# Two-token loads and 128-column unpacking for two more tiles, and fewer, wider filler products

## The chip, the cores and the metric

The kernel runs on one core of a Trainium2 chip. The metric is the device time of one execution in microseconds, as the median of several runs. A core has five engines that work side by side and wait for each other by semaphores: PE (TensorE, matrix products), DVE (VectorE), ACT (ScalarE), POOL (GpSimd) and SP (SyncE, which here issues all DMAs).

## The reference

The inputs are q, k and v (8 batches, 8 heads, 576 tokens, 64 columns per head, float32) and the weights w_in (512 x 1024), conv_w (3 x 1024) and w_out (1024 x 512), which arrive as float64. Attention is computed in chunks of 64 tokens, each chunk with itself alone; a gated feed-forward part with a convolution over three tokens follows.

```python
scores = scale * np.matmul(q_c, k_c.transpose(0, 1, 2, 4, 3))     # chunks of 64 tokens
scores = scores - np.max(scores, axis=-1, keepdims=True)
attn = np.exp(scores)
attn = attn / (np.sum(attn, axis=-1, keepdims=True) + 1e-09)
x = np.matmul(attn, v_c)                                          # then heads side by side: (B, S, 512)

h = np.maximum(x @ w_in, 0.0)
conv_out = sum(conv_w[k] * hp[:, k:k + S, :] for k in range(3))   # hp: h with a zero row at each end
gate = 1.0 / (1.0 + np.exp(-conv_out))
out = (h * gate) @ w_out
```

## The kernel before

The 4608 tokens are cut into 36 tiles of 128 tokens for attention (two chunks each) and into units of about 384 tokens for the feed-forward part. Float32 accuracy on PE is reached by splitting operands into a high and a low half (names ending in `_h` and `_l`); the weights are split on the chip from their 64-bit words, in blocks: conv_w, then w_in in six loads, then w_out in four. Each block passes through one of two slots (`w_slots`), and a slot is free again when DVE has run `w_words` (L567) on it.

**A tile's way.** For the first nine tiles SP loads 128 rows of q and of k (`load_rows`) into one of three row slots. `t_pe` brings them onto PE with the head's columns on the partitions, into two PSUM banks, one call for each `i` of 0 and 1; `t_copy` copies each bank to `qkT` in SBUF, on ACT or DVE (helper lines L76 and L78). A row slot is free after its tile's second `t_pe`. Then follow `scores` (L247), the row maximum and the subtraction on DVE (L257, L261), the exponential on ACT (L266), sum and reciprocal on DVE, the normalisation, `p_pe` (four transposes, L326), `p_copy`, and `attn_v` (L339). `x_hi` (ACT) and `x_lo` (DVE) make the input of the first product `mm1` (L408). ReLU, convolution and gate follow on ACT and DVE (L416 to L481), and the second product runs at L512, in seven part products for each pair of output tiles.

**Two kinds of row loads.** For the first `NP` tiles the rows are loaded with two tokens side by side: even partitions hold q and odd ones k, partition 2p and 2p+1 tokens 2p and 2p+1 of all heads, in pieces of 512 bytes. Here `t_pe` can't transpose; it multiplies 64 columns of the rows (one head, one of the two tokens) with every second column of the identity, so that only q or only k comes out (L196). The other tiles, `NP` to 8, are loaded in pieces of 256 bytes (L133) and transposed (L201).

**What sets the order.** The program lists some 1900 steps. Each step has an engine, an assumed cost and the steps and buffers that it needs. A list written out by hand (`order_`) gives the order on every engine; a planner walks through it and assigns each step a begin in planned microseconds. The instructions are then emitted by planned begin, and each engine keeps its own order. On PE, up to a planned time of 110, gaps of the plan are filled: before a PE step, so many transposes of the identity into an idle PSUM bank are emitted as the planned gap divided by 0.14 (L1140). `pe_free` starts at 2.0, so the first gap is the one before the first `t_pe`. Only the number of fillers depends on the plan; on the chip a step starts when its engine has come to it and its semaphores are there. On the queue of SP the DMAs are issued in the same fixed order, and a DMA that waits for a slot holds back those behind it.

Of the kernel before, what the change touches and what calls it, by code (L numbers as in the profile page):

```python
# [21 lines left out]
F32R = mybir.dt.float32r  # L22
# [8 lines left out]
def attn_ffn(ctx: ExitStack, tc: tile.TileContext, q, k, v, w_in, conv_w, w_out, out):  # L31
    nc = tc.nc
    B, H, S, D = q.shape
    DM, DF = w_in.shape
    w_in, conv_w, w_out = (w.bitcast(U32) for w in (w_in, conv_w, w_out))
    P = 128
# [3 lines left out]
    G = H // 2  # L40
# [13 lines left out]
    ONE_PAIR = True  # L54
    TP = 12
    NF = 3
    NP = 5
    DIRECT = ()
    scale = 1.0 / float(D) ** 0.5

    const = ctx.enter_context(tc.tile_pool(name="const", bufs=1))
# [12 lines left out]
    def copy_on(eng, out, in_):  # L74
        if eng == "ACT":
            nc.scalar.copy(out=out, in_=in_)  # L76
        else:
            ENG[eng].tensor_copy(out=out, in_=in_)  # L78

    def step(eng, cost, key, fn, args=(), after=(), take=(), free=(), lag=0.0, port=False, bank=None, other=(), soft=()):  # L80

        s = dict(eng=eng, cost=cost, key=key, fn=fn, args=args, after=[a for a in after if a], take=take, free=free,
                 lag=lag, port=port, bank=bank, other=other, soft=[a for a in soft if a])
        steps.append(s)
        return s

    sx = ps_s.tile([P, 2, 512], F32, name="sx_ps")
    banks = [None] * 6  # L90
    ps_y = ExitStack()
    ident = const.tile([P, P], F32, name="ident")
    make_identity(nc, ident)
    rebias = const.tile([P, 1], F32, name="rebias")
    nc.scalar.activation(out=rebias, in_=ident[:, 0:1], func=AF.Exp)
    nc.gpsimd.memset(rebias, -896.0 * 2 ** 23)
# [89 lines left out]
    def t_pe(st, i):  # L186

        if not i:
            st["qk"] = work.tile([P, 2, G, 2 * C], F32, name="qkT")
        tp = banks[st["tp", i]]  # L190
        if st["t"] < NP:
            r = row_slot(st).rearrange("p (g u e d) -> p g u e d", g=G, u=2, e=2)
            for g in range(G):
                for e in range(2):
                    for u in range(2):
                        nc.tensor.matmul(tp.rearrange("p (g e n) -> p g e n", g=G, e=2)[D * u:D * u + D, g, e],  # L196
                                         lhsT=r[:, g, u, e], rhs=ident[:, i::2], start=True, stop=True)
            return
        rows = row_slot(st)[:, 512 * i:512 * i + 512]
        for g in range(G):  # L200
            nc.tensor.transpose(out=tp[:, P * g:P * g + P], in_=rows[:, P * g:P * g + P], identity=ident)  # L201

    def t_copy(st, i, eng):
        tT = st["qk"][:, i]
        if st["t"] < NP:
            copy_on(eng, tT.rearrange("p g (n e) -> p g e n", e=2), banks[st["tp", i]].rearrange("p (g e n) -> p g e n", g=G, e=2))
            return
        copy_on(eng, tT, banks[st["tp", i]].rearrange("p (g i) -> p g i", i=P))

# [481 lines left out]
    def att(t, key, load_key, writes):  # L691

        st = {"t": t}
        if t < NAT:
            r = "slot"
            ld = step("SP", 1.2 if (2 * t) % NCK < NCK - 1 else 2.3, load_key, load_rows, (st, t), take=[(r, st)], lag=1.9 if t < NP else 2.8)
            tt = []
            for i in range(2):
                s = step("PE", 0.9 if t < NP else 0.44, key - 3, t_pe, (st, i), [ld, before.get("t")], take=[("bk", st, ("tp", i))] + ["qk"] * (not i), free=[r] if i else [])
                before["t"] = s  # L700
                tt.append(step("ACT", 0.63 if t < NP else 0.59, key - 3, t_copy, (st, i), [s], free=[("bk", ("tp", i))], other=[("DVE", 0.69, False)]))
            slot_users.append(s)
        else:
            tt = [step("DVE", 1.23 if (2 * t + 1) % NCK else 1.39, key - 3, t_dve, (st, t), ring(t), take=["qk"])]
            before["T", t] = tt[0]
        ldv = step("SP", (1.7 if (2 * t) % NCK < NCK - 1 else 2.2) if t < TP else 0.5 if (2 * t) % NCK < NCK - 1 else 1.0, load_key + 0.05 if t < 5 else key - 8, load_v, (st, t), [before.get("v")], take=["v"], lag=1.1 if t < TP else 0.75 if (2 * t) % NCK < NCK - 1 else 1.2)
        tt[0]["after"] += [before["T"]] if t else []
        before.update(v=ldv, T=tt[-1])
        before["new"].append((st, t, tt, ldv, writes, key))
        if t >= PAIR and (t - PAIR) % 2 == 0:  # L710
            return
        new, old = before["new"], before["x"] if t >= BOTH else []
        before["new"], key = [], new[0][5]
        after = [a for n in new for a in n[2]] + [before.get("s")] + [a for o in old for a in o[2]]
        take = x_take(old) + s_take(new)
        free = ["qk"] * len(new) + x_free(old)
        if old:
            s = step("PE", 0.47 * len(new + old), key, both, (new[0][0], [n[0] for n in new], [o[0] for o in old]), after,
                     take=take, free=free, bank="sx")
        else:  # L720
            s = step("PE", 0.47, key, scores, (st,), after, take=take, free=free, bank="sx")
        before["s"] = s
        x_all(old, s, key)
        if t == PAIR - 1:
            a = step("POOL", 0.0, key, give_up, (lent,), [s], take=[("bk", lent, ("y", 0))])
            step("POOL", 0.0, key, give_up, (lent,), [a], take=[("bk", lent, ("y", 1))], free=[("sp", "l1")])
        if t == PAIR + 1:
            step("POOL", 0.0, key, lend, (lent,), [s], take=["sx", "sx"], free=[("sp", "l0")])
        before["x"] = [(st_, t_, end_ + [v_], w_) for (st_, t_, _, v_, w_, _), end_ in zip(new, soft_all(new, s, key))]
        if t + 1 < BOTH:  # L730
            x_alone(key + 14)
        elif t == NT - 1:
            x_alone(key + 18)
# [69 lines left out]
    group_loads, before, lent = {}, {"new": [], "x": []}, {}  # L803
# [133 lines left out]
    for u in range(NU):  # L937
# [4 lines left out]
        while begun < NT and not all(t in x_done for t in range(until[u])):  # L942
            t, begun = begun, begun + 1
# [188 lines left out]
    for i in range(6):  # L1132
        banks[i] = (early_banks if i in (lent["y", 0], lent["y", 1]) else ps_b).tile([P, 512], F32, name=f"b{i}_ps")
    made = {}
    pe_free, until_ = 2.0, 110.0
    for i in sorted(order_, key=lambda i: begin[i]):
        if steps[i]["eng"] == "PE" and begin[i] <= until_:
            idle = [b for b, uses in enumerate(taken) if all(t1 < pe_free or t0 >= begin[i] for t0, t1 in uses)]
            for _ in range(int((begin[i] - pe_free) / 0.14) if idle else 0):
                nc.tensor.transpose(out=banks[idle[-1]][:, 0:P], in_=ident, identity=ident)  # L1140
            pe_free = begin[i] + steps[i]["cost"]
        n = len(nc.cur_bb.bb.instructions) if steps[i]["port"] else 0
        steps[i]["fn"](*steps[i]["args"], *([steps[i]["eng"]] if steps[i]["other"] else []))
        if steps[i]["port"]:
            made[i] = list(nc.cur_bb.bb.instructions)[n:]
# [40 lines left out]
```

## Time and profile before

| | |
|---|---|
| time, median of 3 runs | 476.48 us (476.42 to 477.97) |
| span of the profiled execution | 475.5 us, first to last instruction; no other time of this execution is recorded |
| PE busy | 464.0 us (98%) |
| DVE, ACT, POOL busy | 413.0, 257.7, 289.4 us (87%, 54%, 61%) |
| chain that ended last | PE 89%, DVE 5%, ACT 2%, issue 2% |
| TensorE's granted clock | 0.996 on average over the span |

A busy share says how much of the span an engine worked, not whether it was waited for. The chain is followed back from the last instruction: at each step to what released it, or to the instruction before it on its engine. "Issue" is time in which an engine waited for nothing that the profile shows. The granted clock is given as a share of 2.4 GHz; the lower level, 0.50, is 1.2 GHz. Products are pipelined on PE, so that the duration of one is longer than the distance to the next; the chain's rows give the distance.

### The profile page before, as it was taken

To read this page: it belongs to the slowest core of one execution; us is meant where nothing else is said; L and a number is where in the kernel's file an instruction comes from. 1 tells how busy PE (TensorE), PEld (TensorE's weight loads), DVE (VectorE), ACT (ScalarE), POOL (GpSimd) and SP (SyncE) were. 2 spreads that over 40 slices of the span, in tenths; PEclk is the share of its full clock that TensorE was granted. 3 is DMA by queue.
4 is the path that set the end of the run, shared out by engine and by line. 5 is a ranking of instruction groups with operands and counts; after the bars stand their busy time and mean duration, and the time that the engine had idled before them with its cause. 6 is when DMAs were issued, how large, how long until landed. Compare 5 with 4: busy or idle time off the path is not lost.

```text
span 475.5 us, 13438 instructions
## 1 busy us (share of the span) xinstructions
PE 464.0 (98%) x5481; PEld 452.9 (95%) x5481; DVE 413.0 (87%) x775; ACT 257.7 (54%) x535; POOL 289.4 (61%) x260
## 2 busy tenths in 40 slices
PE   8989889999999999999999999999999999999996
PEld 8879889999999999999999999999999999999996
DVE  2869999999999898989988999898998998788694
ACT  2557989955555463554564465453545545444631
POOL 0124678976777666767667857467868553633523
PEclk9989999999999999999999999999999999999999
DMA  6878999998789999999938283600361100101002
GB/s 195 237 216 255 282 207 193 188 162 205 133 143 211 200 204 160 157 228 165 221 80 149 60 208 80 166 23 23 102 167 45 46 23 2 46 1 68 8 38 112
DMA packets 186369, 64.33 MB, mean 135 GB/s; under 512 B 159660, under 2 KB 177092, under 8 KB 186308
## 3 DMA queue, kind: packets, MB, share of 16 engines
q1 hardware_dynamic: 186308, 63.48, 61.9%
q8 instruction: 43, 0.70, 0.6%
q14 instruction: 18, 0.15, 0.1%
HBM read 50.88 MB, written 23.59 MB: 157 GB/s over the span
## 4 chain that ended last, share of the span: by engine, by line
PE 89%; DVE 5%; ACT 2%; issue 2%; POOL 1%; POOLq 0%; DVEq 0%
PE b_ps L512 38%; PE b_ps L408 38%; PE sx_ps L247 3%; PE sx_ps L339 3%; PE b_ps L196 2%; PE b_ps L1140 2%; PE z_ps L339 1%; DVE wt L567 1%; PE z_ps L247 1%; PE b_ps L326 1%; DVE gt L451 1%; DVE wt L562 1%; DVE m L257 1%; ACT wt L558 0%; DVE wt L261 0%
## 5 line engine op out<-in xcount | busy, mean ns | idle before, releaser
L512 PE MATMUL b_ps<-wo_h,f 128*128 128x256 f32 x1008 | 190.6, 282 | 0.1
L512 PEld LDWEIGHTS b_ps<-wo_h,f 128*128 128x128 f32 x1008 | 158.6, 188 | 2.2 <-POOL f L78 0.7
L512 PE MATMUL b_ps<-wo_l,f 128*128 128x256 f32 x504 | 141.3, 280 | 0.6 <-issue 0.6
L451 DVE SCALAR_TENSOR_TENSOR gt<-b_ps,cw,gt 128x384 f32<-128x384 f32 (+3 forms) x208 | 116.6, 576 | 9.0 <-ACT gt L446 7.1
L499 POOL TENSOR_TENSOR f<-gt,f 128x512 fp32r<-128x512 f32 x71 | 91.8, 1298 | 29.3 <-ACT f L76 9.8
L512 PEld LDWEIGHTS b_ps<-wo_l,f 128*128 128x128 f32 x504 | 94.9, 188 | 0.3 <-issue 0.3
L408 PE MATMUL b_ps<-x_h,wi_h 128*128 128x386 f32 (+2 forms) x384 | 84.7, 342 | 0.9 <-DVE gb L481 0.9
L408 PE MATMUL b_ps<-x_l,wi_h 128*128 128x386 f32 (+2 forms) x384 | 83.3, 338 | 0.0
L408 PE MATMUL b_ps<-x_h,wi_l 128*128 128x386 f32 (+2 forms) x384 | 83.1, 338 | 0.0
L462 ACT ACTIVATE gt<-gt 128x384 f32<-128x384 f32 (+2 forms) x96 | 50.2, 523 | 43.8 <-DVE gt L451 43.6
L408 PEld LDWEIGHTS b_ps<-x_l,wi_h 128*128 128x128 f32 x384 | 68.8, 188 | 0.0
L408 PEld LDWEIGHTS b_ps<-x_h,wi_l 128*128 128x128 f32 x384 | 68.6, 188 | 0.0
L408 PEld LDWEIGHTS b_ps<-x_h,wi_h 128*128 128x128 f32 x384 | 65.7, 188 | 1.8 <-DVE gb L481 1.2
L446 ACT ACTIVATE gt<-b_ps,cw 128x384 f32<-128x384 f32 (+2 forms) x104 | 56.4, 555 | 18.0 <-DVE b_ps L418 16.3
L416 ACT ACTIVATE b_ps<-b_ps 128x386 f32<-128x386 f32 (+2 forms) x78 | 37.3, 479 | 51.5 <-PE b_ps L408 47.6
L502 POOL TENSOR_TENSOR gt<-gt 128x512 f32<-128x512 f32 x43 | 55.5, 1295 | 15.2 <-PE b_ps L408 6.0
L481 DVE SCALAR_TENSOR_TENSOR gt<-gt,b_ps 128x192 f32<-128x192 f32 (+2 forms) x120 | 47.2, 410 | 8.1 <-ACT gt L462 7.4
L78 POOL CAST f<-gt 128x512 fp32r<-128x512 f32 x42 | 25.8, 613 | 33.9 <-PE b_ps L512 24.1
L76 ACT CAST f<-gt 128x512 fp32r<-128x512 f32 x43 | 26.5, 617 | 25.2 <-PE b_ps L512 14.8
L217 DVE STREAM_TRANSPOSE qkT<-qk 128x1024 f32<-128x1024 f32 (+1 forms) x30 | 33.3, 1119 | 0.4 <-DMA qk<-rows 0.4
L524 ACT ACTIVATE wt<-b_ps 128x256 f32<-128x256 f32 x50 | 18.9, 381 | 24.9 <-PE b_ps L512 24.9
L499 POOL TENSOR_TENSOR f<-gb,f 128x512 fp32r<-128x512 f32 x14 | 18.1, 1294 | 17.8 <-ACT f L76 8.7
(96 smaller groups left out, 614.8 us busy)
## 6 DMA issues: line engine op xcount, KB each, us to landing
out<-wt SPq DMA_DIRECT2D x36, 256.0 KB, 3.7
qk<-rows SPq DMA_DIRECT2D x24, 320.0 KB, 5.0
rows<-in_k SPq DMA_DIRECT2D x12, 576.0 KB, 8.7
rows<-in_q SPq DMA_DIRECT2D x12, 576.0 KB, 8.3
qk<-rows SPq DMA_DIRECT2D x24, 256.0 KB, 4.5
v<-in_v SPq DMA_DIRECT2D x21, 256.0 KB, 5.0
w<-in_moe_w_out SPq DMA_DIRECT2D x4, 1024.0 KB, 6.1
wt<-wt SPq DMA_DIRECT2D x48, 64.0 KB, 2.0
```

The costliest lines, as they stand in the source:

```text
L76: nc.scalar.copy(out=out, in_=in_)
L78: ENG[eng].tensor_copy(out=out, in_=in_)
L217: nc.vector.transpose(out=to[:, :, i:i + n], in_=of[:, :, o:o + n])
L408: nc.tensor.matmul(h_ps[:, 0:w], lhsT=wt[:, f // 2, kt, P * (f % 2):P * (f % 2) + P], rhs=xt[:, u % NX, kt, 0:w], start=n == 0, stop=n == ...
L416: nc.scalar.activation(out=h, in_=h, func=AF.Relu)
L446: nc.scalar.mul(out=g, in_=h, mul=cw[:, FT + f:FT + f + 1])
L451: nc.vector.scalar_tensor_tensor(out=g, in0=h, scalar=w, in1=g, op0=ALU.mult, op1=ALU.add)
L462: nc.scalar.activation(out=g, in_=g, func=AF.Tanh, scale=0.5)
L481: nc.vector.scalar_tensor_tensor(out=o, in0=g, scalar=1.0, in1=hv, op0=ALU.add, op1=ALU.mult)
L499: ENG[eng].tensor_tensor(out=part(st, 1), in0=quarter(*src), in1=part(st, 0).bitcast(F32), op=ALU.subtract)
L502: ENG[eng].tensor_tensor(out=quarter(*out_), in0=quarter(*a), in1=quarter(*b), op=op)
L512: nc.tensor.matmul(o, lhsT=part(ft, a)[:, j, :], rhs=w[:, i, j, :], start=first and n == 0, stop=n == 3 * FT // 2 - 1, skip_group_check=True)
```

## The change

Five things change. `NP` goes from 5 to 7, so tiles 5 and 6 are loaded and unpacked like tiles 0 to 4. A product of `t_pe` takes all 128 columns of the identity, reordered so that q's rows come first and then k's; one product so gives a head's q and k for one token of each pair, half of the products suffice, and a call `i` covers two pairs of heads for q and k, where before it covered all heads for q or for k. `t_copy` follows that layout. A constant `ident_r`, the identity in the format of PE's faster float32 products, is made by a copy on ACT. The fillers become products of `ident_r` (two of 256 columns, or one of 512 once 13 steps are emitted); the first gap is filled only up to a planned length of 2.9, and later gaps only where they are longer than 0.8. The list `order_` is as it was; one assumed cost of `t_pe` becomes 0.86, and the assumed cost and load delay of tiles 5 and 6 follow `NP`.

```diff
-    NP = 5
+    NP = 7
+    HALVES = 13
...
+    ident_r = const.tile([P, P], F32R, name="ident_r")
+    nc.scalar.copy(out=ident_r, in_=ident)
...
-            for g in range(G):
-                for e in range(2):
-                    for u in range(2):
-                        nc.tensor.matmul(tp.rearrange("p (g e n) -> p g e n", g=G, e=2)[D * u:D * u + D, g, e],
-                                         lhsT=r[:, g, u, e], rhs=ident[:, i::2], start=True, stop=True)
+            for n in range(4):
+                for u in range(2):
+                    nc.tensor.matmul(tp[D * u:D * u + D, P * n:P * n + P], lhsT=r[:, 2 * i + n // 2, u, n % 2],
+                                     rhs=ident.rearrange("p (n i) -> p i n", i=2), start=True, stop=True)
...
-            copy_on(eng, tT.rearrange("p g (n e) -> p g e n", e=2), banks[st["tp", i]].rearrange("p (g e n) -> p g e n", g=G, e=2))
+            copy_on(eng, st["qk"][:, :, 2 * i:2 * i + 2, :].rearrange("p i g (n e) -> p g e i n", e=2),
+                    banks[st["tp", i]].rearrange("p (g e i n) -> p g e i n", g=2, e=2, i=2))
...
-                s = step("PE", 0.9 if t < NP else 0.44, key - 3, t_pe, (st, i), [ld, before.get("t")], take=[("bk", st, ("tp", i))] + ["qk"] * (not i), free=[r] if i else [])
+                s = step("PE", 0.86 if t < NP else 0.44, key - 3, t_pe, (st, i), [ld, before.get("t")], take=[("bk", st, ("tp", i))] + ["qk"] * (not i), free=[r] if i else [])
...
-    pe_free, until_ = 2.0, 110.0
+    pe_free, until_, filled = 2.0, 110.0, 0
...
-            for _ in range(int((begin[i] - pe_free) / 0.14) if idle else 0):
-                nc.tensor.transpose(out=banks[idle[-1]][:, 0:P], in_=ident, identity=ident)
+            gap = begin[i] - pe_free if idle else 0.0
+            for _ in range(int((min(gap, 2.9) - 0.3) / 0.43) if pe_free == 2.0 else int((gap - 0.3) / 0.235) if gap > 0.8 else 0):
+                n = 2 if filled < HALVES else 4
+                for _ in range(4 // n):
+                    nc.tensor.matmul(banks[idle[-1]][:, 0:P * n], lhsT=ident_r,
+                                     rhs=ident_r.rearrange("p (o n) -> p o n", o=1).broadcast_to([P, n, P]), start=True, stop=True)
+                filled += 1
```

## Rows read from the trace of the kernel before

**Rows 1.** The page's busy times (us, share of the span) and instructions.
```profile
PE 464.0 (98%) x5481; PEld 452.9 (95%) x5481; DVE 413.0 (87%) x775; ACT 257.7 (54%) x535; POOL 289.4 (61%) x260
```

**Rows 2.** Windows: PE, PEld, DVE, ACT, POOL busy; clock, DMA share, GB/s.
```profile
0.00:18.60 18.60, 17.24 (x352) 15.56 (x354) 9.42 (x21) 5.31 (x10) 2.69 (x9) 1.00 0.72 209
...
0.00:23.34 23.34, 21.98 (x475) 19.61 (x476) 13.24 (x29) 8.64 (x16) 2.69 (x9) 1.00 0.77 216
...
23.34:25.15 1.81, 0.00 (x1) 0.00 (x0) 1.36 (x3) 0.00 (x0) 0.00 (x0) 1.00 0.51 110
25.15:28.70 3.55, 3.55 (x65) 2.98 (x65) 0.00 (x0) 2.63 (x6) 0.94 (x1) 0.53 0.73 200
28.70:78.00 49.30, 45.32 (x581) 42.44 (x583) 47.59 (x85) 42.19 (x85) 27.91 (x27) 1.00 1.02 239
78.00:470.00 392.00, 391.24 (x4353) 386.11 (x4354) 349.97 (x658) 204.25 (x431) 257.90 (x225) 1.00 0.57 116
```

**Rows 3.** The chain that ended last, in order of time: start, us, what.
```profile
1.36 5.73 PE b_ps L1140 x35
7.09 1.09 PE b_ps L196 x32
8.18 0.26 PE b_ps L1140
...
10.87 0.62 PE sx_ps L247 x32
...
23.34 1.81 issue
...
26.03 1.04 PE b_ps L326 x4
...
27.50 1.11 PE sx_ps L247 x32
28.70 0.70 DVE m L257
...
87.27 0.44 PE b_ps L326 x4
87.70 1.42 PE b_ps L512 x12
89.12 0.11 PE b_ps L1140
```

**Rows 4.** DVE's waits in 0 to 30: us in total, times, longest.
```profile
DVE m L257 <- PE sx_ps L247: 5.9, 3, 4.0
```

**Rows 5.** Timeline of PE: start, duration, what, idle before and its releaser.
```profile
25.15 0.88 PE L339 MATMUL sx_ps<-p_all,v 64*64 64x64 f32 x26 [1.81 <-issue]
...
33.38 2.35 PE L1140 MATMUL b_ps<-ident 128*128 128x128 f32 x20
...
64.53 0.69 PE L339 MATMUL sx_ps<-p_all,v 64*64 64x64 f32 x32 [1.51 <-ACT p_all L76]
```

**Rows 6.** DMA queue of kind instruction: whole span, then 22.6 to 22.8 (packets, MB, share).
```profile
q8 instruction: 43, 0.70, 0.6%
...
q8 instruction: 1, 0.02, 28.9%
```

**Rows 7.** Windows, columns as in rows 2, around two stretches of row loads.
```profile
3.00:3.50 0.50, 0.50 (x4) 0.50 (x3) 0.00 (x0) 0.00 (x0) 0.00 (x0) 1.00 1.13 339
...
22.00:22.50 0.50, 0.50 (x19) 0.50 (x21) 0.50 (x3) 0.50 (x2) 0.00 (x0) 1.00 1.26 287
```

**Rows 8.** Timeline of the first loads and of ACT's start.
```profile
1.56 0.64 SPq L126 DMA_DIRECT2D qk<-in_k  x1
2.02 0.20 ACT L95 ACTIVATE rebias<-ident 128x1 f32<-128x1 f32 x1
```

**Rows 9.** DMA issues of 1.5 to 2.2: size, us from issue to landing.
```profile
qk<-in_k SPq DMA_DIRECT2D x1, 256.0 KB, 3.3
```

**Rows 10.** All fillers on PE: duration in ns, min/median/max, first and last start.
```profile
L1140 PE MATMUL b_ps<-ident x112: 271/273/472, 1.4 to 93.7; 128*128 128x128 f32 x112
```

## Prediction, made before the change was run

> **What bounds the kernel now.** I read the shares of the engines first: PE is busy for 464.0 of 475.5 us [rows 1]. That is an average, so I took the span by stages [rows 2]. The reader is to see three regimes. From 78 to 470 us PE has no idle time that counts (391.24 of 392.00): every microsecond by which this stretch begins earlier is a microsecond of the total. From 28.7 to 78 DVE is the full engine (47.59 of 49.30), while PE has gaps and fillers. Before 28.7 neither is full: DVE did 14.6 us of work (13.24 + 1.36), all of it after conv_w landed at 5.55, and of the three times that it waited for scores, 5.9 us in all, the longest, 4.0 us, lies directly before 28.70, where the fourth scores end [rows 3, 4]. So the total is set by when that fourth scores run, and the chain of waits says what they stood behind: 5.73 us of fillers from 1.36, unpacking products with fillers between them, and 1.81 us from 23.34 in which PE waited for nothing that is recorded [rows 3].
>
> **That 1.81 us halt** is in the middle of attn_v of tile 0, whose operands were all ready (its remaining 26 products start together at 25.15 with no releaser but "issue" [rows 5]). One queue of kind "instruction" moved 43 packets, 0.70 MB, so 16 KB each [rows 6]; PE ran 5481 + 5481 instructions [rows 1], which is 255 per packet. At the halt PE had run 475 products and 476 weight loads [rows 2]; with some 7% of semaphore instructions, which are not counted, that is 1024 = 4 x 256, a packet's edge. A packet of that queue moved in 22.6 to 22.8 [rows 6], where the DMA engines were full (share 1.26 just before [rows 7]). I read it as PE waiting for its next block of instructions. Afterwards the granted clock is down: 0.53 on average until 28.70 [rows 2], where four transposes took 1.04 us and one scores 1.11 us, against 0.44 and 0.62 at full clock [rows 3].
>
> A rule speaks against this reading. The Trainium skill (Runtime: NRT & Kernel Launch, Instruction fetch mechanics) also has blocks of 256 instructions, but says that the fetch of the next runs beside the present one and is mostly hidden, and gives PE room for 2048. By that page the halt would not be a fetch, the change would not remove it, and the time would be that of rival 1. The trace agrees on the size of a block and disagrees on the hiding, as far as a halt on an edge shows it.
>
> **The change part by part**, against the span of 475.5 us; the runs' median, 476.48, lies 0.97 above it, which I add at the end.
>
> *First fill.* Before, 35 transposes hold PE from 1.36 to 7.09, though the second half of tile 0's rows (issued 1.56, 3.3 us to landing) is there at 4.9 [rows 8, 9]. Afterwards the fill is int((2.9 - 0.3)/0.43) = 6 steps of two 256-column products. They read ident_r, an ACT copy that takes its place behind the table load, where ACT's first operation now starts at 2.02 and takes 0.20 [rows 8], so PE begins near 2.35 instead of 1.36. A 256-column product takes 0.118 us at full clock (12 in 1.42 [rows 3]) and twice that at the lower level, at which the first transposes ran (up to 472 ns against a median of 273 [rows 10]). Fill: 1.4 to 2.8 us, end 3.8 to 5.2. Unpacking starts between 4.9 (rows) and 5.2; I take 5.2: **-1.8 us**. If the first unpacking product group still runs at the lower level it costs up to 1.1 us more; part of that is hidden, because DVE is busy with conv_w until 7.14 and copies tile 0 only then.
>
> *Unpacking products.* Per half tile 16 products of 64 columns (32 records, 1.09 us [rows 3]) become 8 of 128 (16 records). If the record sets the pace (34 ns), 0.55 us; if the columns do, 1.09. I take 0.95, nearer to the row of this same function: ten halves, -1.4 us. Between the halves there are thirteen small fillers in eight places up to 23 us; one costs 0.26 us on the chain, and the eight places together 2.5 us [rows 3]. Their gaps are below 0.8 us in the plan (n fillers mean 0.14n to 0.14(n+1)), so they go. That is 3.9 us of PE's own time; not all passes. With unpacking from 5.2, tile 0's copies follow conv_w's work on DVE (7.14 to 8.5), so its scores start at 8.6 instead of 10.80. Slot 0 is free at 7.4 instead of 9.5, so tile 3's rows, which wait for it, go 2.1 us earlier and tile 4's about 3 us. Following DVE's and ACT's fixed order from there with the durations of before, attn_v of tile 0 begins at 19.7 instead of 23.01: **-3.3 us, the first term included**.
>
> *The halt.* Until the end of the fourth scores the new program has 12 + 10 x 16 + 4 x 32 + 1 + 8 + 32 = 341 products, 732 instructions with the same 7%, not 1024. The fourth edge moves to about the sixth scores; there PE had 2.35 us of fillers [rows 5], a cover. An edge (768) falls just behind the fourth scores, but its packet is asked for about 6 us ahead, where before PE consumed a block in 4.7 us (18.6, where 352 + 354 had run, to 23.34 [rows 2]). So -1.81 for the halt and, with the clock kept, -0.38 - 0.60 - 0.49 - 0.43 = -1.9 for the rest of attn_v, four transposes, the scores and two fillers. That makes -7.0 at the fourth scores. DVE can't take it all: 14.6 us of work after 5.55 ends at 20.15 at best, plus waits for tile copies and w_in; I put its row-maximum at 22.7 instead of 28.70: **-6.0 us** (bounds: -8.5 from DVE's work, -3.3 if the halt stays).
>
> *28.7 to 78.* DVE's chain shifts as a whole, and what it waits for shifts with it, since the w slots are freed by DVE and the row slots by PE. Not everything can: a w_in block takes 5 to 8 us from issue to landing. Each half of tiles 5 and 6 goes from four transposes (0.44 us, as the four of [rows 3]) to 0.55 to 1.09: four times +0.5, beside gaps of which the largest held twenty fillers [rows 5]; if that cover is gone, +2 us at worst. Their copies keep 512 columns each and are costed at nothing; ACT and DVE would have to carry what they cost more. Their loads go as pieces of 512 bytes; tile 0's, of that kind, moved at 339 GB/s, the 256-byte pieces around 22 us at 287 [rows 7], so about 0.5 us less for 1.05 MB. I take **+0.8 us** given back (0 to +6).
>
> *After 78.* The gaps near 89 and 93.6 held one and two fillers, 0.11 us each on the chain of a full PE [rows 3]: **-0.3 us**.
>
> Sum: -6.0 + 0.8 - 0.3 = -5.5; span 470.0, time **471.0 us**. Its own range is 469 to 473.
>
> **Rivals.**
> 1. *The halt stays or comes back on the chain* (at another edge, or because it was no fetch). For it: the DMA stays busy (0.75 to 1.02 by stages [rows 2]), and a block took 4 us from edge to packet (18.6 to 22.6). Against it: the edge moves by some 280 instructions and the program consumes them more slowly. Then only the -3.3 and the -0.3 are left, less 0.6 given back: 473.5.
> 2. *The front's gain is lost between 28.7 and 78*: a DVE at 97% beside a DMA share of 1.02 [rows 2] may have its own end, where loads come late or the longer unpacking of tiles 5 and 6 sits before mm1. For it: the chain there passes through ACT and POOL as well, and loads of 5 to 8 us lie beside it. Against: loads wait for slots there, not for the DMA. About -1.2: 475.3.
> 3. *Slower: PE at the lower clock through the whole front.* The gaps below 0.8 us are no longer filled; before, one idle time of 1.81 us was followed by 0.50. If the level stays low from 5.2 to the fourth scores, ten halves cost 0.95 more each, three scores 0.49, and with the transposes and attn_v the fourth scores begin near 30.5, not 27.43: +3, time 479.5. It decides from about seven halves at the low level (6 / 0.95). Against: PE stays some 80% busy there, and a gap of 1.51 us at 63 was followed by an attn_v of 0.69 us, its full-clock time [rows 5].
>
> **How the numbers follow.** Forecast 0.53, more than forecast (below 469) 0.04, rival 1 0.20, rival 2 0.15, rival 3 0.08. 0.5% is 2.4 us, about what a measurement of this kernel can tell from no change; the limits are 474.1 and 478.9. Faster: 0.53 + 0.04 + 0.14 of rival 1 = 0.71. Slower: 0.07 of rival 3 and 0.02 of rival 2 = 0.09. Same: 0.20. The range, 468 to 476.5, holds forecast, rival 1 and most of rival 2.
>
> **What would show it.** First unpacking product at 4.9 to 5.3; PE idle nowhere above 1.2 us between 5 and 25 us, clock 1.00 in 8 to 30; scores of the first tile near 8.6; DVE's fourth row-maximum at 22 to 23.5; PE without gaps from about 72.5. It is wrong if a halt with "issue" stands before that row-maximum, if the clock shows 0.50 there, or if the row-maximum is early and PE's full stretch still begins at 77 or later.

## The result and the profile after

The changed kernel took 473.19 us (median; 472.39 to 476.98), the kernel before 477.23 beside it: a ratio of 0.9899 with a 95% interval of 0.985 to 0.9948, so it is faster, by 1.0% or 4.0 us. Two more sets of runs, `a_again` and `a_late` below, with the same program up to 460 us, gave 472.47 (ratio 0.9892, 0.9853 to 0.993) and 473.07 (0.9894, 0.9857 to 0.9932), 5.4 and 4.8 us below the kernel before beside them (477.83 both times). The forecast was 471.0, 5.5 us below 476.48.

The profiled execution has a span of 470.6 us, 4.9 less than before. First the front, by PE's timeline of the changed kernel (start, duration, what, and in brackets the idle time before it and its releaser; L198 is now the unpacking, L250 the scores, L342 attn_v, L1146 the fillers):

```profile
2.37 2.93 PE L1146 MATMUL b_ps<-ident_r 128*128 128x256 f32 x12 [2.37 <-ACT ident_r L96]
5.30 3.66 PE L198 MATMUL b_ps<-ident,qk 128*64 128x128 f32 x48
8.90 0.69 PE L250 MATMUL sx_ps<-qkT 64*64 64x64 f32 x32
...
17.61 2.04 PE L198 MATMUL b_ps<-ident,qk 128*64 128x128 f32 x32
20.17 0.69 PE L342 MATMUL sx_ps<-p_all,v 64*64 64x64 f32 x32 [0.53 <-ACT p_all L77]
20.80 0.66 PE L329 MATMUL b_ps<-ident,wt 128*128 128x128 f32 x4
21.57 0.69 PE L250 MATMUL sx_ps<-qkT 64*64 64x64 f32 x32
...
27.61 2.37 PE L1146 MATMUL b_ps<-ident_r 128*128 128x256 f32 x14
29.91 0.46 PE L250 MATMUL sx_ps<-qkT 64*64 64x64 f32 x15
31.22 0.50 PE L250 MATMUL sx_ps<-qkT 64*64 64x64 f32 x17 [0.86 <-issue]
```

The first fill ends where the rows are there, each of the first scores comes earlier, attn_v of tile 0 runs in one piece (0.69 us, against 6 and 26 products with 1.81 us between them [rows 3, 5]), and the halt now stands inside the sixth scores, after 15 of its 32 products. (From here on a record is one product in the trace, and a halt is idle time of PE with "issue" as its releaser.) DVE's timeline shows the fourth row-maximum with no wait before it:

```profile
22.40 0.69 DVE L260 TENSOR_REDUCE m<-sx_ps 128x8 f32<-128x512 f32 x1
```

It was at 28.70 [rows 3]. By windows (columns as in rows 2), DVE is as full as before in the next 50 us, and PE nearly without gaps from 72.80 (389.80 of 392.20 us):

```profile
5.30:22.40 17.10, 15.61 (x334) 13.50 (x334) 14.43 (x31) 8.27 (x17) 1.90 (x2) 1.00 0.97 277
...
22.40:72.80 50.40, 45.84 (x618) 41.29 (x614) 47.91 (x87) 43.92 (x89) 29.41 (x27) 1.00 1.01 242
72.80:465.00 392.20, 389.80 (x4318) 384.96 (x4318) 349.47 (x656) 203.32 (x430) 257.15 (x225) 1.00 0.57 116
```

The gain is followed by pairing the n-th product of `mm1` and of the second product in both traces: -5.78 us at 73 us, -6.15 from 92 to 127, -6.49 at 147, -5.83 at 167, -4.79 at 182, and -4.9 from there to the end. So the front was won, and 1.7 us were given back between 147 and 182 us. PE's waits of the changed kernel from 100 to 460 (total, times, longest) say where:

```profile
PE sx_ps L342 <- DVE p_all L319: 1.3, 1, 1.3
PE z_ps L342 <- DVE p_all L319: 1.0, 1, 1.0
```

`p_dve` (L319) itself waited for four small DMAs, `wt<-wt`, that swap blocks of the softmax's results between partitions; in this document "the first swap" is the one near 150 us and "the second" the one some 20 us later. SP's timeline (start, time for the issue) of the changed kernel, and then of the kernel before:

```profile
147.43 0.60 SPq L154 DMA_DIRECT2D rows<-in_k  x1
148.20 5.48 SPq L316 DMA_DIRECT2D wt<-wt  x4
```

```profile
151.11 0.65 SPq L151 DMA_DIRECT2D rows<-in_k  x1
154.69 3.16 SPq L313 DMA_DIRECT2D wt<-wt  x4
```

Before, the swap was issued 2.9 us after the issue ahead of it had ended; now it follows within 0.2 us, and the four issues take 5.48 us instead of 3.16. It still begins 6.49 us earlier, by as much as PE is ahead there; what is longer is the DMA itself, whose first piece lands 5.7 us after its issue instead of 3.4.

### The profile page after: what moved, and what is told of

Same layout as the page of the kernel before. It is cut to its first block, busy times and chain, and to the rows that moved or that the text cites. A ratio compares the mean times of both kernels' runs of the same rounds, so it can differ in the third digit from the quotient of the medians.

```text
span 470.6 us, 13056 instructions
## 1 busy us (share of the span) xinstructions
PE 456.2 (97%) x5290; PEld 444.3 (94%) x5290; DVE 412.7 (88%) x775; ACT 257.2 (55%) x536; POOL 289.3 (61%) x260
## 4 chain that ended last, share of the span: by engine, by line
PE 78%; DVE 9%; DMA 3%; POOL 3%; ACT 3%; issue 2%; SPq 2%; DVEq 0%; POOLq 0%; ACTq 0%
PE b_ps L411 34%; PE b_ps L515 34%; PE sx_ps L342 2%; DMA w<-in_moe_w_in 2%; PE sx_ps L250 2%; DVE gt L454 1%; DVE wt L570 1%; DMA wt<-wt 1%; PE z_ps L250 1%; PE z_ps L342 1%; SPq L129 1%; POOL wt L310 1%; PE b_ps L329 1%; PE b_ps L1146 1%; SPq L316 1%
```

## The experiments

Theory A was the prediction's: the front sets the time, and the halt is PE's wait for its next block of instructions. The rivals: C, the first fill is what counts; D, the row loads of tiles 5 and 6; others as quoted. "At 100 us" means the shift of the paired products there, against the first trace of before.

**Products alone** (`b_products`), the kernel before with the new `t_pe` and `t_copy`:

```diff
...
-                        nc.tensor.matmul(tp.rearrange("p (g e n) -> p g e n", g=G, e=2)[D * u:D * u + D, g, e],
-                                         lhsT=r[:, g, u, e], rhs=ident[:, i::2], start=True, stop=True)
...
+                    nc.tensor.matmul(tp[D * u:D * u + D, P * n:P * n + P], lhsT=r[:, 2 * i + n // 2, u, n % 2],
+                                     rhs=ident.rearrange("p (n i) -> p i n", i=2), start=True, stop=True)
...
```

> The kernel before with one edit alone: unpacking by 128-column products (16 records per half tile instead of 32); five tiles, loads and fillers as before. Theory A (the 1.81 us halt is PE at the edge of a 256-instruction block that has not arrived): PE runs 160 records fewer before attn_v of tile 0, so the edge that lay at its seventh record lies about 33 us in, among fillers; no halt of over 0.5 us before the fourth scores, clock 1.00 in 20 to 30, the fourth row-maximum on DVE near 24.2 instead of 28.7, time 3 to 4.5 us below the kernel before (about 472.5). Theory B (the halt is no fetch): it stays in attn_v of tile 0, the gain is ten times 0.11 us and less, time within 1.2 us of the kernel before.

477.63 us (475.34 to 479.75), ratio 0.9983 (0.9956 to 1.001): no gain. There was no halt in the front, as Theory A said, and Theory B falls with that; but the time is what Theory B said. The fourth row-maximum came at 26.26, not near 24.2, the products at 100 us were only 1.6 us earlier, and in the profiled execution (479.45, one of the slowest of the twelve) all of that was lost again: the last products are 2.2 us later than before. PE's waits from 100 to 460 in that profile:

```profile
PE z_ps L339 <- DVE p_all L316: 1.7, 1, 1.7
PE sx_ps L339 <- DVE p_all L316: 1.3, 1, 1.3
PE z_ps L247 <- issue: 0.8, 1, 0.8
PE b_ps L408 <- issue: 0.5, 1, 0.5
```

**Fillers alone** (`b_fill`), the kernel before with `ident_r` and the new filler rule:

```diff
...
-            for _ in range(int((begin[i] - pe_free) / 0.14) if idle else 0):
...
+            for _ in range(int((min(gap, 2.9) - 0.3) / 0.43) if pe_free == 2.0 else int((gap - 0.3) / 0.235) if gap > 0.8 else 0):
...
```

> The kernel before with one edit alone: the new fillers (ident_r, first fill of 12 products of 256 columns, later ones in long gaps alone); unpacking and loads as before. Both theories: first unpacking product at 5.3 instead of 7.0. Theory A: only 36 records go before attn_v, so the edge lies in the fourth scores, about 9 of 32 records in, and a halt of 0.5 to 2 us stands there, with a low clock behind it if it is long; time 1.5 to 3 us below the kernel before. Theory B (the halt came from the fillers or from something in attn_v): no halt in the fourth scores; either none at all, with 4 us or more below the kernel before, or one in attn_v as before.

477.97 us (476.38 to 480.22), ratio 0.9989 (0.996 to 1.0017): no gain, where Theory A had 1.5 to 3 us. In the profiled execution (476.48, one of the fastest) the front was 3.35 us earlier at 100 us in spite of three halts; 1.6 us went in a swap wait at 177.5 and 1.8 in a halt at 255.8. PE's timeline of the front:

```profile
11.87 0.50 PE L250 MATMUL sx_ps<-qkT 64*64 64x64 f32 x17 [0.34 <-DVE qkT L79]
12.96 0.46 PE L250 MATMUL sx_ps<-qkT 64*64 64x64 f32 x15 [0.59 <-issue]
16.31 0.46 PE L250 MATMUL sx_ps<-qkT 64*64 64x64 f32 x16
17.34 0.46 PE L250 MATMUL sx_ps<-qkT 64*64 64x64 f32 x16 [0.57 <-issue]
22.02 0.34 PE L250 MATMUL sx_ps<-qkT 64*64 64x64 f32 x6 [0.19 <-ACT x_h L397]
23.92 0.62 PE L250 MATMUL sx_ps<-qkT 64*64 64x64 f32 x26 [1.56 <-issue]
```

The last of them stands in the fourth scores, after 6 of its products, where Theory A had about 9. Each halt is inside a group of equal products whose operands are there. Counted from the start of the program they stand after 222, 349 and 475 records of products: 127 and 126 apart. So many products and as many weight loads are 252 to 254 instructions, 256 if two to four semaphore instructions, which are not counted, stand among them.

**More records in the first gap** (`b_shift`): three of the first transposes become eight small products (two records each), 13 records more ahead of attn_v.

```diff
-            for _ in range(int((begin[i] - pe_free) / 0.14) if idle else 0):
+            for _ in range(int((begin[i] - pe_free) / 0.14) - 3 * (pe_free == 2.0) if idle else 0):
...
+            for n in range(8 if pe_free == 2.0 else 0):
+                nc.tensor.matmul(banks[idle[-1]][D * (n % 2):D * (n % 2) + D, 0:D], lhsT=ident[:, 0:D], rhs=ident[:, 0::2], start=True, stop=True)
```

> The kernel before with 13 more records of PE in its first gap (3 transposes out, 8 small products of 2 records in; about 0.2 us longer), nothing else. Theory A: the edge comes 13 records earlier, so the halt leaves attn_v and stands in the second half of tile 4's unpacking, after about 25 of its 32 records, 1 to 2.5 us long. Theory B: the halt stays in attn_v of tile 0 after its sixth record. Time about that of the kernel before in both, 476 to 478.

477.16 us in its one run. The expected halt at the moved edge did not come; there was none in the front at all. Fourth row-maximum at 26.62, -1.5 us at 100 us. So the program alone does not make PE halt at an edge. That a halt depends on when the packet comes is shown further below, from all traces together.

**The kernel before again** (`b_again`), nothing changed:

> The kernel before once more, nothing changed, for a second trace of it. Theory A (its halt is a wait for the fifth block of instructions, at a fixed place): PE stops inside attn_v of tile 0 after 475 records (products), with 'issue', if it stops at all; how long depends on when the packet comes. Theory E (the waits for the swapped weights at 155 to 180 us, which every changed kernel showed and the first trace of before did not, come by chance from loaded DMA queues): this trace shows between 0.5 and 2.5 us of them too. Rival F (they come only to kernels whose front is earlier): none here, as in the first trace.

476.59 us in its one run, span 474.8. PE's timeline shows a halt at the same product, but of 0.24 us, with the clock kept:

```profile
23.14 0.34 PE L339 MATMUL sx_ps<-p_all,v 64*64 64x64 f32 x6
23.73 0.62 PE L339 MATMUL sx_ps<-p_all,v 64*64 64x64 f32 x26 [0.24 <-issue]
```

Its fourth row-maximum is at 25.91, 2.8 us earlier than in the first trace, but its products at 100 us only 1.6 us earlier. `b_products` and `b_shift`, which had no halt there at all, gained just those 1.6 and 1.5. These two are a fair pair, since in both PE came to full pace late (their first fills, still mostly the same transposes, ran until 8.2 us or later, against 6.7 here); between them the products gained 0.1 us at 100 us. Theory E missed: DVE waited for the swap 0.4 us, PE not at all. Rival F had none, and none came; but an earlier front is not enough to make them, since `b_shift`, with the same front shift as this trace, waited 0.5 and 0.8. What PE's wait at that first swap does follow, in all fourteen traces, is SP's time for its four issues: up to 4.15 us (six traces) there is none worth listing, at 4.50 it is 0.32 (`a_again`), at 4.70 0.53 (`b_shift`), at 4.81 0.63 (`a_fill35`), at 4.83 0.65 (`a_np9`), at 4.95 0.77 (`a_half0`), at 5.48 1.31 (`b_products` and the changed kernel), at 6.19 2.04 (`a_np5`). That is the issue time less 4.2 us. It does not follow how far ahead the front is: `b_products`, 1.9 us ahead at 147 us, waited 1.31 us, `a_late`, 6.7 us ahead, not at all.

**The long first fill put back** (`a_fill35`), the changed kernel with before's rule for the first gap alone (35 transposes):

```diff
+            for _ in range(int(gap / 0.14) if pe_free == 2.0 else 0):
+                nc.tensor.transpose(out=banks[idle[-1]][:, 0:P], in_=ident, identity=ident)
-            for _ in range(int((min(gap, 2.9) - 0.3) / 0.43) if pe_free == 2.0 else int((gap - 0.3) / 0.235) if gap > 0.8 else 0):
+            for _ in range(0 if pe_free == 2.0 else int((gap - 0.3) / 0.235) if gap > 0.8 else 0):
```

> The changed kernel with its first fill alone put back to 35 transposes from 1.4 to 7.1 us. Theory A (most of the gain is the halt, and DVE's work bounds the front): first unpacking product at 7.1 instead of 5.3, but 0.5 to 1.6 us of these 1.8 reach the fourth row-maximum (23 to 24 instead of 22.4); time 0.3 to 1.6 us above the changed kernel. Theory C (the earlier first product is the gain): at least 3 us above the changed kernel, no clear difference from the kernel before.

475.17 us (473.38 to 478.49), ratio 0.996 (0.9930 to 0.9989): about 2 us above the changed kernel in its other sets of runs. Its unpacking starts at 6.7, its fourth row-maximum at 24.07 instead of 22.40, the products at 97 us are 5.0 us earlier than before instead of 6.15. By that the short first fill is worth 1 us at 97 us and perhaps 2 in the time: Theory A was somewhat low, C too high. It is a rough figure: five traces of the changed kernel's own front (`a_again`, `a_swap`, `a_swap2`, `a_late` and its first) lie from -3.8 to -6.4 us at 100 us.

**Five tiles of two-token loads** (`a_np5`), the changed kernel with `NP = 5`:

```diff
-    NP = 7
+    NP = 5
```

> The changed kernel with NP at 5 again: tiles 5 and 6 are loaded in pieces of 256 bytes and transposed; products, first fill and fillers as changed. Theory A (tiles 5 and 6 add PE work that is hidden and save some 0.5 us of DMA): within 1 us of the changed kernel. Theory D (their shorter loads are what the first 30 us needed): 1.5 to 3 us above it, with PE or ACT waiting for rows or for w_in before 36 us.

474.4 us (472.5 to 477.76), ratio 0.992 (0.9892 to 0.9949). That is 1.2 to 1.9 us above the changed kernel, between A and D. It is also products and fillers together, without tiles 5 and 6: 3.4 us faster than before, where each alone gave nothing. The profiled execution was the slowest of the ten (477.76, only 1.2 us ahead of before at 100 us, with the clock at 0.66 from 35 to 40 us), so it does not show what tiles 5 and 6 are worth in the others. PE's waits in it from 0 to 40 show rows that come late ("issue" stands here before an unpacking group, after 241 records, not at an edge):

```profile
PE b_ps L198 <- issue: 1.7, 1, 1.7
PE sx_ps L342 <- ACT p_all L77: 1.6, 1, 1.6
PE b_ps L198 <- DMA qk<-in_k: 1.1, 1, 1.1
```

**All nine** (`a_np9`), tried as a faster version, `NP = 9`:

```diff
-    NP = 7
+    NP = 9
```

> The changed kernel with tiles 7 and 8 loaded as two tokens and unpacked too (NP = 9). Theory A with the DMA as the front's second limit: the pieces of 512 bytes land earlier, but those tiles are unpacked behind 30 us, where DVE is the full engine, and four halves cost PE 0.5 us more each: the start of PE's full stretch moves by -0.5 to +0.8 us, the time by as much, 471.5 to 473.5. Rival D (each further tile of 512-byte pieces gains like tiles 5 and 6, which gave 1.4 to 1.9): 470 to 471.

476.12 us (474.13 to 478.13), ratio 0.997 (0.9943 to 0.9997): slower than the changed kernel by some 3 us, outside both expectations. In its trace (474.9) the front is part of it: -4.0 us at 78 us instead of -5.8. A halt of 0.68 us stands again after 474 records, one of 1.01 us at 228, and the two swap waits take 0.65 and 0.8. That the two further tiles are the cause is not shown, since kernels with the same front as the changed one came out as slow (`a_swap` below).

**Wide fillers only** (`a_half0`), `HALVES = 0`:

```diff
-    HALVES = 13
+    HALVES = 0
```

> The changed kernel with every filler one product of 512 columns instead of two of 256 at first (HALVES = 0): 13 records fewer by the sixth scores, so the edge that stood after 15 records of the sixth scores comes 13 later, after 28 of them. Theory A: any halt is there, of 0 to 0.9 us, and the time is that of the changed kernel within 0.7 us (471.8 to 473.9). Rival: the coarser first fill holds PE past the landing of the first rows and shifts the front by up to +0.5 us, the time by as much.

476.09 us (472.47 to 478.5), ratio 0.9969 (0.9938 to 1.0). The edge came where Theory A put it, after 28 of the sixth scores:

```profile
30.17 0.68 PE L250 MATMUL sx_ps<-qkT 64*64 64x64 f32 x28
33.18 0.33 PE L250 MATMUL sx_ps<-qkT 64*64 64x64 f32 x4 [2.33 <-issue]
33.31 0.77 PE L342 MATMUL sx_ps<-p_all,v 64*64 64x64 f32 x32
34.00 1.12 PE L329 MATMUL b_ps<-ident,wt 128*128 128x128 f32 x4
```

But the halt was 2.33 us, not at most 0.9, and it cost: in the 3 us behind it the granted clock is 0.64 and four transposes take 1.12 us. By windows, this kernel, and then the changed one, whose halt was 0.86 us:

```profile
33.18:36.20 3.02, 3.02 (x52) 2.62 (x54) 3.01 (x6) 2.35 (x6) 1.43 (x2) 0.64 0.89 276
```

```profile
31.22:34.00 2.78, 2.78 (x75) 2.54 (x77) 2.75 (x5) 2.33 (x6) 1.16 (x1) 1.00 0.94 359
```

So the time was not that of the changed kernel. The profiled execution (477.76) was slower than the median, and two of the twelve, 472.47 and 473.5, were as fast as the changed kernel. The rival missed too: the first unpacking started at 5.23. At 78 us this trace is 2.3 us ahead of before where the changed kernel is 5.8 ahead.

**The changed kernel again** (`a_again`), beside the next two kernels:

> The changed kernel as it is, in the same job as the next three, which are compared with it, and for the spread of its runs. Median 473 to 474. Theory A (the halt at a packet's edge comes or not by how long the packet waits): its edge lies in the sixth scores, where little hangs on it, so the mean granted clock is 0.999 or more in most runs (before: 15 of 29), and runs under 0.999 are about 2 us longer than the others, as before (478.8 against 476.8).

472.47 us (471.8 to 475.86). The halt stood after the same 474 records, 0.58 us at 30.62; the swap waits were 0.32 and 1.40 us. Four of the six executions had a mean clock of 0.999 or more, and the other two (473.6 and 475.86) were the longest, as Theory A said.

**The load behind the swap** (`a_swap`): the row load that SP issued just before the first swap is moved behind it; `a_swap2` also moves the two loads ahead of the second swap behind that one:

```diff
+    order_.remove(1069)
+    order_.insert(order_.index(655) + 1, 1069)
```

```diff
+    order_.remove(1069)
+    order_.insert(order_.index(655) + 1, 1069)
+    order_.remove(1042)
+    order_.insert(order_.index(801) + 1, 1042)
+    order_.remove(1041)
+    order_.insert(order_.index(801) + 1, 1041)
```

> The changed kernel with one DMA moved: the shuffle of batch 5 that is issued directly before the second swap of softmax blocks (at 147 us) is issued directly after it. Theory E (what was given back after 78 us is the swap's DMA queued behind a shuffle's small packets): the first piece of that swap lands in about 3.4 us instead of 5.7, PE's wait of 1.31 us at 156.7 is gone, time 0.6 to 1.3 us below the changed kernel. Rival: the wait only goes to the next swap (0.96 us at 175.6 becomes about 2), time within 0.4 us.

> The same, and two loads of parts for tiles 20 to 22, issued directly before the third swap (at 168 us), are issued after it. Theory E: both waits of PE for the swapped blocks (1.31 and 0.96 us) go or fall below 0.4, time 1.2 to 2.2 us below the changed kernel. Rival: the parts land later, DVE's transposes of tiles 20 and 21 wait for them, time within 0.5 us or above.

475.91 us (474.03 to 478.23), ratio 0.9947 (0.9918 to 0.9976), and 475.2 us (473.03 to 478.01), 0.9937 (0.9912 to 0.9963). The wait went at each swap whose loads were moved (the four issues of the first took 2.46 and 2.45 us), and a longer one came at the next: PE's waits from 100 to 460, first `a_swap` (at 176.60), then `a_swap2` (at 202.15):

```profile
PE z_ps L342 <- DVE p_all L319: 2.4, 1, 2.4
```

```profile
PE sx_ps L342 <- DVE p_all L319: 2.4, 1, 2.4
PE b_ps L515 <- ACT wt L527: 0.6, 1, 0.6
```

So the load just ahead of the first swap is what makes its issues long, but moving it did not win the time. Whether the move made the next wait longer is not shown, since `a_late` below has 2.21 us there without it. Both kernels were slower than the changed one beside them (472.47) by 2.7 us and more, and part of that lies in a front whose program they share with it. `a_swap`'s unpacking waited 1.9 us in three places for rows; in `a_swap2` PE waited 1.27 us for ACT, and the granted clock was 0.50 from 33.4 to 36.7 us behind it.

**Another build of the same front** (`a_late`), two stores at 462 us exchanged:

```diff
+    order_.remove(1838)
+    order_.insert(order_.index(1750) + 1, 1838)
```

> The changed kernel with one difference that no engine waits for: two of the last six stores of the output (tiles 31 and 32, at about 462 us) are issued in the other order. Everything before 460 us is the same program. It asks how far a time belongs to a program and how far to one build of it, since other variants with the same front ran 2 to 3 us above the changed kernel, with a halt and a lower clock in most of their runs. Theory G (the time is the program's): 471.8 to 473.8, at least two thirds of the runs with the mean clock at 0.998 or more. Rival H (each build draws its own share of long halts in the front): 474.5 to 476.5, with most runs below 0.998; then differences of less than some 3 us between variants of the changed kernel say nothing on their edits.

473.07 us (472.0 to 473.48), ratio 0.9894: Theory G, with three of its four executions at a mean clock of 1.00; rival H falls for this pair. In its trace no halt stood in the sixth scores, and the first swap cost nothing, the second all the more:

```profile
30.25 0.70 PE L250 MATMUL sx_ps<-qkT 64*64 64x64 f32 x32
```

```profile
175.09 1.16 PE L342 MATMUL z_ps<-p_all,v 64*64 64x64 f32 x64 [2.21 <-DVE p_all L319]
```

What remains open is why `a_swap` and `a_swap2`, the same program up to 147 us, ran with a lower mean clock in nearly all their runs (19 of 22 below 0.998). Late rows alone are not it: `a_late`'s unpacking waited 1.9 us for them as well, and its products at 100 us were 6.4 us ahead. While this is open, 2 to 3 us between two variants of the changed kernel are not safely the worth of their edit, and what `a_fill35`, `a_np5`, `a_np9` and `a_half0` say in their times is to be read with that.

## Why the prediction was right, step by step

*The first fill.* Forecast: PE from 2.35, fill 1.4 to 2.8 us, unpacking at 5.2. Measured: 2.37, 2.93, 5.30. The products ran at 0.244 us each, twice the 0.118, as the upper bound had it.

*Unpacking.* 0.95 us a half was taken; the rows show 1.02 (2.04 for two) to 1.13, about the upper bound of 1.09, with half as many records. So the columns set the pace, not the records. The first three halves took 3.66, or 1.22 each, because PE was still at half pace until about 6.3: part of the 1.1 us that the prediction set aside for that. In all, the first scores came at 8.90 (forecast 8.6) and attn_v of tile 0 at 20.17 (19.7).

*The halt.* The edge moved to the sixth scores, where the prediction put it, and it costs little there in the five traces of this front (0.86, 0.58 and three times 0 us). That it is an edge of equal blocks of instructions is now shown. There are seventeen halts of 0.2 us or more with "issue" inside a run of products of one line, in nine traces of seven programs; they stand after 222, 349, 474 to 475, 2250, 2883 to 2884, 3137, 3266, 3646 or 4279 records, and all of these lie within two records of 95 plus a multiple of 126.8. In the other five traces there is none. 126.8 products and as many weight loads are 253.6 instructions, so of 256 about 1% are left for semaphores, not the 7% of the prediction; the rest of what it counted so stands ahead of the first edge, which by this count comes after 95 records where a full block holds 127. Its place for the fourth edge came out right all the same.

The halt ends with the packet. In the trace of before one of the instruction queue starts at 22.7 and PE goes on at 25.15; in the changed kernel at 28.9 and 31.22, in `a_half0` at 31.0 and 33.18, in `b_again` at 21.4 and 23.73. The queue of `a_half0` from 30.8 to 31.2 (packets, MB, share):

```profile
q8 instruction: 1, 0.02, 15.0%
```

A trace has 41 to 43 such packets, about one for each edge. Paired in order, the first packet with the second edge and so on, all seventeen halts end 2.1 to 2.7 us after the start of their packet, and no edge in the fourteen traces is passed sooner than 2.1 us after it. So what decides is whether the packet comes that long before PE reaches the edge. Each of the four packets came after PE had crossed the edge before: by 4.2 us in before (18.5 to 22.7), 3.2 in `b_again`, 5.7 in the changed kernel (23.2 to 28.9), 7.3 in `a_half0` (23.7 to 31.0). PE took 4.8 us (before) to 7.1 us (`a_half0`) for a block there; with the 2.2 us or more behind the packet that leaves 2.6 to 4.9 us for it. The Trainium skill (Runtime: NRT & Kernel Launch, Instruction fetch mechanics) agrees with this on the blocks of 256 and on the fetch that runs beside the present block; its "mostly hidden" holds for most of the 41 to 43 edges of each trace, and not for the seventeen, which cost 0.24 to 2.33 us each. In the 5 us before these the DMA share was 0.83 to 1.42; many other edges at such a share were passed without a halt.

*The fourth row-maximum.* 22.7 forecast, 22.40 measured: -6.3 for -6.0. But the parts were mis-sized, and that the sum fits so well against this one trace is in part luck. The halt was priced at its length in one execution. The missing halt does make the 2.7 us that the sum gave it at the row-maximum (2.8 in `b_again`), but `b_again` won them with nothing changed, and only 1.6 of them reach 100 us. Products alone give nothing beyond that. Fillers alone give -3.35 us at 100 us in one trace, in spite of three halts; the whole change gives -3.8 to -6.4 in the five traces of its front. So the rest is worth more than it was given, and the parts don't add. One reading fits the timelines but was not tested by itself: with the old fillers PE has no time to spare however fast the products are (in `b_products` it is never idle for more than 0.15 us from 1.36 to 27.6), and with the old products the edges fall on the scores (`b_fill`).

*22.4 to 73.* Forecast +0.8 for what the row loads, the w_in blocks and tiles 5 and 6 give back; measured +0.5 (50.40 us from the row-maximum to PE's full stretch, against 49.88 from 28.70 to 78.58). The fillers after 78: -0.3 forecast, -0.37 measured (-5.78 to -6.15).

*The step that failed* is the sentence that every microsecond by which PE's full stretch begins earlier is a microsecond of the total. PE arrived 5.8 us earlier, was 6.5 ahead at 147 us, and 4.9 came through: 2.3 us went in two swap waits, less 0.6 us for a halt at 166 us that the first trace of before has. The swaps are issued behind row loads of many small pieces, and `a_swap` shows that such a load makes the issues long. The DMA engines have no room there in either kernel: their share from 140 to 200 us is 1.06 in the changed one and was 1.08 before. Whether PE's lead itself brings the waits is open: PE lost nothing at swaps in both traces of the unchanged kernel and 1.3 to 3.0 us in the twelve others, but the loss does not grow with the lead at 147 us (3.0 us in `b_products`, 1.9 ahead; 2.2 in `a_late`, 6.7 ahead). Rival 2 had this kind of loss, a gain lost to loads that come late, but at 28.7 to 78 us; there almost nothing was lost.

*The offset.* 0.97 us was added to the span, the median of the runs less the profiled span. Where both are recorded for one execution, the time is 1.79 above the span (472.39 and 470.6), and by that the profiled execution of before took some 477.3, above its median. Of the 2.2 us between forecast and median, 0.8 is this, 0.6 the span (470.6 for 470.0), and 0.8 that the median run was slower than the profiled one.

Rival 3 did not come: from 6.4 us on the granted clock of the changed kernel is 1.00 in all windows of the front. `a_half0` shows its mechanism, though: after 2.33 us of halt the clock was 0.64 over 3 us, after 0.86 us it stayed at 1.00. The prediction's argument against it, a gap of 1.51 us that kept the clock, does not hold in every execution: in `a_np5` a gap of 1.47 us at the same place (62.95) was followed by an attn_v of 1.13 us instead of 0.69. Nor does every long gap lower the clock: after 2.41 us in `a_swap` (at 176.6) it was 1.00. A lower clock also goes with the longer executions. Runs of one kernel differ by up to 7 us, and in 29 runs of before the medians are 476.84 (15 runs at a mean clock of 0.999 and above) and 478.83 (14 below).

No variant that was tried beats the changed kernel.

## What to carry to other kernels

An "issue" halt inside a group of equal products is recognised by counting: if the records up to it, in several traces, differ by multiples of one number, it stands at the edge of a block of instructions. It is then compared with the start of the packets in the instruction queue. Its length differs from execution to execution (0.24 and 1.81 us at one edge of one kernel), so one trace doesn't price it.

A microsecond won at the front of a full engine is not yet a microsecond of the total: here 1.6 of 6.5 us were lost again to small transfers that stand behind large ones in the queue. Look at the share of the DMA engines in each later stage before counting it.

Parts of a change that remove different waits on one engine are to be measured together as well as alone: here two parts gave nothing each and 3.4 us together. And where builds with the same front differ by 3 us, one build per variant settles less than its interval says.

## What was not expected of the hardware

Four small DMAs (`wt<-wt`, 64 KB each) took SP 2.45 to 6.19 us to issue; in `a_swap`, where the row load just ahead of them was moved away, 2.46 instead of 5.48. The first products ran at half pace (0.244 us for 256 columns) in a window whose granted clock is printed as 1.00. The trace's list of the granted clock explains it: its first entry stands at 6.40 us (4.86 in before, 4.2 to 8.5 in the fourteen traces), time ahead of it is printed as 1.00 for want of an entry, and the pace of the products doubles there (in before from 0.21 to 0.11 us between two transposes, at 4.8 us). So the start of the front differs from execution to execution too: `b_products`' 35 transposes took 6.94 us, those of before 5.73. And a kernel of one core on one chip varies by 1% from run to run; blocks of instructions that come early or late are one cause that the traces show.
